# Sink attention and two mixture layers on one core: one float32r product for the sinks, one more Strassen pair, other queues at both ends

## The chip, the core and the metric

The kernel runs on one core of a Trainium2 chip. TensorE (PE) multiplies matrices into PSUM, VectorE (DVE) and ScalarE (ACT) work elementwise on SBUF and PSUM, GpSimd (POOL) elementwise on SBUF alone, and SyncE (SP) issues DMAs; ScalarE and GpSimd can issue DMAs too. The metric is the device time of one execution in microseconds.

## What is computed

Per head of 64 columns, 768 positions attend to the first 4 positions (the sinks) and to a causal window of 128; two layers with different activations follow, each of two products. Everything is float32.

```python
scores = scale * np.matmul(q, k.transpose(0, 1, 3, 2))       # (2, 8, 768, 768)
keep = is_sink | in_window                                    # pos < 4, or 0 <= rel < 128
scores = np.where(keep, scores, -1000000000.0)
a = softmax(scores); attn = np.matmul(a, v)
x = attn.transpose(0, 2, 1, 3).reshape(B * S, H * D)          # 1536 x 512
h = x @ w_in                                                  # 512 -> 2048
g = np.where(h >= 1, h, np.where(h <= -1, 0.0, (h + 1) ** 2 / 4))
x = g @ w_out                                                 # 2048 -> 512
h = x @ w2_in; g = h * np.clip(h + 3.0, 0.0, 6.0) / 6.0
out = g @ w2_out
```

## The kernel before

**Precision.** The large products run in float32r, which streams one column per step but keeps fewer bits than float32. So each operand is split into a high part (rounded to float32r) and a low part (what is left), and three products hi x hi, hi x lo and lo x hi are added in PSUM (`product`, line 678; `y_group`, line 857). `high` (line 134) and `low` (line 142) make the parts; for `high`, and for PSUM copies, a planner of costs (`Balance`) picks VectorE or ScalarE when the program is written.

**Order.** The instructions of PE and SP stand in the order in which the program is written (line 915). VectorE, ScalarE and GpSimd are ordered by a scheduler that simulates the timeline; `keep_in_program_order` pins single instructions, and `tick`/`defer` put pieces of work some steps later.

**Attention** (`build_fast_attention`, line 346). Queries go in blocks of 128. A unit is one block of one pair of heads; 48 units in 16 pieces `j` (4 groups times 4 head pairs). `score` (line 421) multiplies q and k on PE in float32, VectorE adds the mask and takes the maximum (line 444), ScalarE takes the exponential with its sum (line 478). After every second unit `normalise` (line 454) inverts the sums of both units (four columns: two units, two heads) and scales the four probability tiles in place: three on GpSimd (line 469), the fourth on ScalarE or VectorE (lines 471, 473); only in the last four units two or more leave GpSimd. From the third block of a batch on a tile has 260 columns: the block before, 4 sink columns, the block itself. There VectorE first writes the scaled sink columns of the four tiles to `psk` (line 459, 128 x 16). Four units later `turn` (line 500) transposes the probabilities on PE, `sinks` (line 518) transposes `psk` to 8 rows (2 heads times 4 sinks), and `mix` (line 526) multiplies: first the sinks, `vs` against `tsink` in float32 (line 536), then the blocks (line 552). `vs` holds the sinks' rows of v, 8 x 1024, zero where a row belongs to the other head; `load_sinks` (line 400) clears and loads it with four DMAs on SP. Twelve of the 16 `mix` calls have a sink product: eight with 256 columns, four with 512.

**Layers.** 1536 tokens are three chunks of 512 columns (`c`), the 2048 hidden units 16 blocks of 128 (`fc`), two blocks a pair (`p`). `h_group` (line 705) makes one block of one chunk with 12 products, `y_group` one block's share of the output with 12. In plain pairs all three chunks are made so. In the others (`paired`, line 772; from `PLAIN[m]` on, 2 in both layers `m`) chunk 0 is made so, and chunks 1 and 2 with Strassen's seven half products of six instructions each. That needs sums of weight quarters (`combine`, line 286) and of quarters of x (`combine_x`, line 729, tiles `x32`), split into high and low parts in deferred steps on VectorE and ScalarE; in the second layer ScalarE copies the quarters from PSUM (line 882). The weights come as pairs of 32-bit words and are narrowed by VectorE and ScalarE (`narrow`, line 184). Chunks 1 and 2 of all hidden blocks go to HBM and come back (`spill`, `fetch`); their `y_group` calls end each layer.

**Both ends.** `begin` (line 565) issues the loads of q, k and v on SP, in line 394 and 395 for piece 0 in two parts each; GpSimd makes the identity (line 917) and the masks (line 356). In the last `y_group` calls ScalarE and VectorE take turns in copying four output banks (lines 890, 892), and SP stores each (line 894).

## Time and profile before

| | us |
|---|---|
| median of three runs | 610.7 (610.14 to 611.74) |
| the profiled execution | 610.59 |
| its span, first to last instruction | 608.8 |

The page lists how long each engine was busy, divides the span into slices, and follows the chain of work that ended last back from the last instruction. It gives PE 91% of that chain, ScalarE 4% and VectorE 3%. Attention runs to about 106 us, the first layer to about 352, the second to the end. An engine named behind `<-` is what ended an idle time. Durations of matmuls are longer than their distance, since they are pipelined; the chain shows the distance.

### The profile page before, as it was taken

The page shows a single profiled execution, that of the slowest core. Times are in us where ns is not written, and L with a number is a line of the kernel's source. Part 1 is how long each engine was busy: PE and PEld are TensorE (multiplying, and loading weights), DVE is VectorE, ACT ScalarE, POOL GpSimd, SP SyncE. Part 2 cuts the span into 40 slices and gives each one's busy share as a digit, 9 for nine tenths or more (in the row PEclk, how much of TensorE's full clock was granted, in tenths as well). Part 3 has the DMA queues.
Part 4 walks back from the last instruction along what each step waited for, and adds up shares of the span by engine and source line. Part 5 has one row for each costly group of instructions (what it writes and reads, how often), then busy time and mean ns, then how long its engine had stood idle before and what let it go on. Part 6 is the DMA issues. An engine that isn't in the chain of part 4 may idle for free.

```text
span 608.8 us, 8222 instructions
## 1 busy us (share of the span) xinstructions
PE 596.7 (98%) x2880; PEld 478.2 (79%) x2880; DVE 466.4 (77%) x852; ACT 391.3 (64%) x700; POOL 104.8 (17%) x152
## 2 busy tenths in 40 slices
PE   7999899999999999999999999999999999999997
PEld 5666566888888888888888888888888888888885
DVE  5777898899897879477798759787787875666652
ACT  5878888586557576586788666665656554455542
POOL 6666661300111101110000000101011110000000
PEclk9999999999999999999999999999999999999999
DMA  5547501984557586767465204365768554963303
GB/s 180 161 134 237 175 23 70 305 282 155 181 187 229 183 232 180 209 198 252 172 237 212 71 15 159 131 214 153 245 163 242 138 186 129 327 250 138 104 1 139
DMA packets 40571, 106.53 MB, mean 175 GB/s; under 512 B 3409, under 2 KB 13137, under 8 KB 40529
## 3 DMA queue, kind: packets, MB, share of 16 engines
q1 hardware_dynamic: 29776, 72.44, 36.9%
q0 software_dynamic: 10752, 33.56, 17.9%
q8 instruction: 23, 0.38, 0.3%
q14 instruction: 20, 0.16, 0.1%
HBM read 69.29 MB, written 34.60 MB: 171 GB/s over the span
## 4 chain that ended last, share of the span: by engine, by line
PE 91%; ACT 4%; DVE 3%; issue 1%; POOL 0%; DMA 0%; SPq 0%; POOLq 0%; ACTq 0%
PE ps_y L874 43%; PE ps_h L682 40%; ACT p L478 3%; PE ps_s L431 2%; PE ps_v L552 2%; DVE p L444 1%; PE ps_t L515 1%; PE ps_v L536 1%; PE ps_t L514 1%; ACT pt L496 0%; DVE xl L145 0%; POOL p L469 0%; DMA kraw<-k_dram 0%; DVE xh L140 0%; PE ps_k L523 0%
## 5 line engine op out<-in xcount | busy, mean ns | idle before, releaser
L874 PE MATMUL ps_y<-gh,wo 128*128 128x512 f32 x768 | 241.8, 390 | 0.0
L874 PEld LDWEIGHTS ps_y<-gh,wo 128*128 128x128 f32 x768 | 144.2, 188 | 29.8
L682 PE MATMUL ps_h<-xh,wi 128*128 128x512 f32 x480 | 155.1, 391 | 0.0
L874 PE MATMUL ps_y<-gl,wo 128*128 128x512 f32 x384 | 149.7, 390 | 0.0
L682 PEld LDWEIGHTS ps_h<-xh,wi 128*128 128x128 f32 x480 | 90.2, 188 | 19.0 <-issue 0.3
L682 PE MATMUL ps_h<-xl,wi 128*128 128x512 f32 x240 | 93.5, 390 | 0.0
L874 PEld LDWEIGHTS ps_y<-gl,wo 128*128 128x128 f32 x384 | 72.1, 188 | 15.4 <-DVE gl L145 0.4
L469 POOL TENSOR_SCALAR p<-p,sm 128x260 f32<-128x260 f32 (+2 forms) x68 | 58.1, 870 | 33.3 <-DVE psk L459 14.7
L138 ACT ACTIVATE gh<-r 128x512 fp32r<-128x512 f32 x64 | 40.1, 629 | 29.3 <-PE ps_y L874 29.2
L478 ACT ACTIVATE p<-p,nm 128x260 f32<-128x260 f32 (+2 forms) x96 | 46.3, 483 | 17.9 <-DVE nm L444 17.7
L145 DVE TENSOR_TENSOR gl<-r,gh 128x512 fp32r<-128x512 f32 x64 | 43.9, 690 | 17.6 <-ACT gh L138 17.4
L682 PE MATMUL ps_h<-xt,st 128*128 128x512 f32 x216 | 52.9, 389 | 0.0
L682 PEld LDWEIGHTS ps_h<-xl,wi 128*128 128x128 f32 x240 | 45.1, 188 | 9.3
L682 PEld LDWEIGHTS ps_h<-xt,st 128*128 128x128 f32 x216 | 40.6, 188 | 8.4
L697 POOL DMA_DIRECT2D h_d<-hq x32 | 17.8, 556 | 136.4 <-ACT hq L138 88.7
L444 DVE CUSTOM_DVE_ANT_0 p<-ps_s,mask 128x260 f32<-128x260 f32 (+2 forms) x96 | 34.5, 396 | 5.4 <-POOL mask L363 3.8
L662 ACT ACTIVATE r<-hq,half 128x512 f32<-128x512 f32 x32 | 22.8, 723 | 24.4 <-DVE gl L145 18.6
L431 PE MATMUL ps_s<-kraw,qraw 64*128 64x260 f32 (+2 forms) x192 | 31.9, 433 | 4.3 <-DMA kraw<-k_dram 4.0
L663 DVE SCALAR_TENSOR_TENSOR r<-r,hq 128x512 f32<-128x512 f32 x32 | 21.8, 691 | 18.5 <-ACT r L662 18.5
L272 POOL DMA_DIRECT2D wo_d<-w x16 | 8.6, 535 | 155.9 <-DVE w L224 155.8
L797 DVE TENSOR_TENSOR hq<-ps_h,p 128x512 f32<-128x512 f32 x36 | 24.8, 688 | 10.6 <-PE ps_h L682 10.4
L145 DVE TENSOR_TENSOR gl<-ps_h,gh 128x512 fp32r<-128x512 f32 x32 | 22.0, 689 | 13.0 <-ACT gh L138 12.9
(104 smaller groups left out, 927.4 us busy)
## 6 DMA issues: line engine op xcount, KB each, us to landing
h_d<-hq POOLq DMA_DIRECT2D x32, 512.0 KB, 6.0
hq<-h_d SPq DMA_DIRECT2D x32, 512.0 KB, 5.5
wo_d<-w POOLq DMA_DIRECT2D x16, 512.0 KB, 7.2
raw1i<-moe_w_in_dram SPq DMA_DIRECT2D x8, 1024.0 KB, 6.9
wr<-wo_d SPq DMA_DIRECT2D x16, 512.0 KB, 4.9
raw1o<-moe_w_out_dram SPq DMA_DIRECT2D x8, 1024.0 KB, 5.6
raw0i<-moe_w_in_dram SPq DMA_DIRECT2D x7, 1024.0 KB, 6.3
raw0o<-moe_w_out_dram SPq DMA_DIRECT2D x7, 1024.0 KB, 5.8
```

Of the source, the lines that this page charges most:

```text
L138: nc.scalar.activation(out=dst, in_=src, func=AF.Copy)
L145: nc.vector.tensor_tensor(out=dst, in0=src, in1=f32(hi), op=ALU.subtract)
L431: nc.tensor.matmul(banks[e], tq[rows, u * P:(u + 1) * P], tk[rows, c0:c0 + w], start=True, stop=True)
L444: nc.vector.tensor_tensor_reduce(out=p[:, e, :], in0=banks[e], in1=masks[min(i, 2)], scale=-SCALE, scalar=BIG, op0=ALU.add, op1=ALU.min, a ...
L469: nc.gpsimd.tensor_scalar_mul(out=px, in0=px, scalar1=r)
L478: nc.scalar.activation(out=p[:, e, :], in_=p[:, e, :], func=AF.Exp, scale=-1.0, bias=nm[:, v + e:v + e + 1], accum_out=sm[:, v + e:v + e + 1],
L662: nc.scalar.activation(out=r, in_=h, func=AF.Relu, scale=1.0 / 6.0, bias=half)
L663: nc.vector.scalar_tensor_tensor(out=g, in0=r, scalar=1.0, in1=h, op0=ALU.min, op1=ALU.mult)
L682: nc.tensor.matmul(ps, a[:, kc, :], b[kc], start=start and i == 0, stop=i == len(ops) - 1, skip_group_check=not start,)
L697: nc.gpsimd.dma_start(out=h_d[m][fc // 2][:, e:e + 2, :], in_=t)
L797: nc.vector.tensor_tensor(out=dst, in0=src, in1=p1, op=ALU.add)
L874: nc.tensor.matmul(ys[dm], a[:, cs], b, start=fc == 0 and i == 0, stop=last and i == 2)
```

## The change

- **Sinks.** The sink rows of v are loaded in three copies per head (24 rows), split once by VectorE (`split_sinks`, a new step) into rows hi, hi, lo. GpSimd instead of VectorE scales the sink columns to `psk` and then writes `psk3` with hi, lo, hi for each tile. The transposes take 24 columns, and the sink product of `mix`, unchanged in its code, is one float32r product of 24 rows.
- **Strassen.** `PLAIN` of the second layer is 1 instead of 2, so its pair `p=1` is `paired`. Two of the four x32 tiles of that layer take buffers of the tag of the narrowed weights.
- **Start.** The two k transfers of piece 0 are issued by ScalarE. GpSimd's work is put in written order: masks, identity, clearing the sinks.
- **End.** The last output bank is copied in halves by ScalarE and VectorE, and stored in halves by ScalarE's and SP's queues.

```diff
-PLAIN = (2, 2)
+PLAIN = (2, 1)
...
                 nc.sync.dma_start(out=tq[:, part], in_=qs[:, part])
-                nc.sync.dma_start(out=tk[:, part], in_=ks[:, part])
+                (nc.scalar if j == 0 else nc.sync).dma_start(out=tk[:, part], in_=ks[:, part])
...
-        vs = at_p.tile([2 * NS, B, DM], F32, name="vs", bufs=1)
+        R = 6 * NS
+        vs = at_p.tile([R, B, DM], F32R, name="vs", bufs=1)
+        third = at_p.tile([P, 1], F32, name="third", bufs=1)
+        vraw = []
 
         def load_sinks():
-            nc.gpsimd.memset(vs, 0.0)
             for b in range(B):
+                t = g_p.tile([P, N], F32, tag="r", name="vsraw", bufs=3)[:R, :DM]
+                vraw.append(t)
+                nc.gpsimd.memset(t, 0.0)
                 for e in range(2):
                     nc.sync.dma_start(
...
+                        out=t[3 * e * NS:3 * (e + 1) * NS, :].rearrange("r (h e d) -> r h e d", e=2, d=D)[:, :, e, :],
+                        in_=v[b, 0:NS, :].rearrange("s (h e d) -> s h e d", e=2, d=D)[:, :, e, :]
+                        .unsqueeze(0).to_broadcast([3, NS, H // 2, D]),
                     )
+
+        def split_sinks():
+
+            nc.vector.tensor_reduce(
+                out=third, in_=ident[:, :R].rearrange("p (e x s) -> p e x s", e=2, x=3)[:, :, 2, :], axis=AX.XY, op=ALU.add
+            )
+            nc.vector.tensor_scalar_mul(out=third, in0=third, scalar1=-1.0)
+            for b in range(B):
+                hi = g_p.tile([P, N], F32R, tag="gh", name="vshi", bufs=3)[:R, :DM]
+                tc.keep_in_program_order(nc.vector.tensor_copy(out=hi, in_=vraw[b]))
+                tc.keep_in_program_order(
+                    nc.vector.scalar_tensor_tensor(
+                        out=vs[:, b, :], in0=f32(hi), scalar=third[:R], in1=vraw[b], op0=ALU.mult, op1=ALU.add
+                    )
+                )
...
-                    nc.vector.tensor_tensor(
+                    ps3 = at_p.tile([P, 4, 3, NS], F32R, tag="psk3", name="psk3", bufs=DIST // 2 + 2)
+                    nc.gpsimd.tensor_tensor(
                         out=ps, in0=p4[:, :, P:KB], in1=sm.unsqueeze(2).to_broadcast([P, 4, NS]), op=ALU.mult
                     )
...
+                if w > 2 * P:
+                    nc.gpsimd.tensor_copy(
+                        out=ps3[:, :, 0:3:2, :], in_=ps.unsqueeze(2).to_broadcast([P, 4, 2, NS])
+                    )
+                    nc.gpsimd.tensor_tensor(out=ps3[:, :, 1, :], in0=ps, in1=f32(ps3[:, :, 0, :]), op=ALU.subtract)
...
-                nc.tensor.transpose(ps[0:2 * NS, n, :], both[:, 2 * NS * n:2 * NS * (n + 1)], ident)
+                nc.tensor.transpose(ps[0:R, n, :], both[:, R * n:R * (n + 1)], ident)
...
             load(0)
-            prepare()
             load_v(0)
             load(1)
             load_v(1)
             load(2)
+            with tc.manual_schedule(engines={mybir.EngineType.Pool}):
+                prepare()
+                make_identity(nc, ident)
             load_sinks()
...
+            if g == 4:
+                steps.append(split_sinks)
...
+        if m and i < 2:
+            if ("a", i) not in x32s:
+                x32s["a", i] = raw_p.tile([P, HK, N], F32, tag="wi32", name=f"x32_{i}", bufs=2)
+            return x32s["a", i]
...
+                        final = c == NCH - 1 and dm == KC - 1
+                        if final:
+                            nc.scalar.activation(out=od[:, :N // 2], in_=ys[dm][:, :N // 2], func=AF.Copy)
+                            nc.vector.tensor_copy(out=od[:, N // 2:], in_=ys[dm][:, N // 2:])
...
+                if m and final:
+                    nc.scalar.dma_start(out=out[cs, c * N:c * N + N // 2], in_=od[:, :N // 2])
+                    nc.sync.dma_start(out=out[cs, c * N + N // 2:(c + 1) * N], in_=od[:, N // 2:])
```

## Rows read from the trace of the kernel before

**Rows 1.** The page's busy line: each engine's busy us, share of span, instructions
```profile
PE 596.7 (98%) x2880; PEld 478.2 (79%) x2880; DVE 466.4 (77%) x852; ACT 391.3 (64%) x700; POOL 104.8 (17%) x152
```

**Rows 2.** Stages: stretch, length, busy us (instructions) per engine, PE clock, DMA, GB/s
```profile
10.00:20.00 10.00, 10.00 (x59) 6.84 (x60) 8.07 (x38) 7.56 (x30) 7.95 (x11) 1.00 0.48 161
...
70.00:80.00 10.00, 10.00 (x80) 6.63 (x78) 8.55 (x33) 7.60 (x26) 8.54 (x10) 1.00 0.15 45
...
90.00:100.00 10.00, 10.00 (x61) 7.20 (x60) 9.54 (x26) 8.29 (x22) 1.77 (x2) 1.00 0.26 105
...
362.00:373.00 11.00, 11.00 (x51) 9.09 (x50) 10.76 (x11) 7.55 (x10) 1.48 (x3) 1.00 0.13 50
```

**Rows 3.** Chain that ended last, whole span: start us, length us, what
```profile
17.58 0.62 PE ps_v L536 x2
...
66.98 2.76 POOL p L469 x3
...
103.48 1.05 PE ps_v L536 x2
...
365.43 2.72 PE ps_y L874 x12
...
604.83 0.69 DVE o L892
```

**Rows 4.** Groups, 5 to 106.4 us, by form: busy us, mean ns | idle before
```profile
L469 POOL TENSOR_SCALAR p<-p,sm 128x260 f32<-128x260 f32 x44 | 41.2, 952 | 26.3 <-DVE psk L459 14.7 <-ACT p L478 7.4 <-ACT pts L496 2.3
...
L469 POOL TENSOR_SCALAR p<-p,sm 128x128 f32<-128x128 f32 x16 | 9.8, 619 | 7.0 <-ACT p L478 3.4 <-PE ps_s L431 2.5 <-ACT pt L496 0.8
...
L536 PE MATMUL ps_v<-pts,vs 8*128 8x256 f32 x16 | 5.4, 419 | 1.4 <-DVE pts L498 0.6 <-ACT pts L496 0.3 <-DVE xl L145 0.3
...
L536 PE MATMUL ps_v<-pts,vs 8*128 8x512 f32 x8 | 4.5, 640 | 0.0
...
L459 DVE TENSOR_TENSOR psk<-p,sm 128x16 f32<-128x16 f32 x16 | 3.2, 202 | 0.4
...
L138 ACT ACTIVATE xh<-ps_v 128x256 fp32r<-128x256 f32 x5 | 1.9, 371 | 0.0
...
L140 DVE CAST wi<-w 128x512 fp32r<-128x512 f32 x2 | 1.1, 557 | 0.1
```

**Rows 5.** Groups, whole span: one scalar-tensor-tensor of VectorE
```profile
L663 DVE SCALAR_TENSOR_TENSOR r<-r,hq 128x512 f32<-128x512 f32 x32 | 21.8, 691 | 18.5 <-ACT r L662 18.5
```

**Rows 6.** Timeline of the start: start us, us, engine, line, op [idle <-releaser]
```profile
0.73 1.28 ACT L478 ACT_TABLE_LOAD   x1 [0.73 <-PEq L1041]
...
2.11 0.43 SPq L395 DMA_DIRECT2D kraw<-k_dram  x1
...
4.50 0.09 POOL L363 MEMSET mask<- 128x4 f32 x1
...
4.79 1.39 PEld L431 LDWEIGHTS ps_s<-kraw,qraw 64*128 64x128 f32 x8 [1.09 <-DMA qraw<-q_dram]
4.83 5.50 PE L431 MATMUL ps_s<-kraw,qraw 64*128 64x256 f32 x20 [0.83 <-DMA kraw<-k_dram]
```

**Rows 7.** Timeline of GpSimd, 60 to 100 us: its longest run
```profile
66.98 8.24 POOL L469 TENSOR_SCALAR p<-p,sm 128x260 f32<-128x260 f32 x9 [3.01 <-ACT p L478]
```

**Rows 8.** Waits, 5 to 106.4 us: total us, times, longest us
```profile
PEld ps_t L514 <- POOL p L469: 4.8, 10, 0.7
```

**Rows 9.** Timeline of VectorE, 352 to 405 us: last two low parts xt
```profile
372.20 1.22 DVE L145 TENSOR_TENSOR xt<-x,xt 128x1024 fp32r<-128x1024 f32 x1
...
383.37 1.23 DVE L145 TENSOR_TENSOR xt<-x,xt 128x1024 fp32r<-128x1024 f32 x1 [0.81 <-ACT xt L138]
```

**Rows 10.** Timelines of ScalarE, then VectorE, 345 to 358 us
```profile
347.11 1.96 ACT L138 ACTIVATE xh<-ps_y 128x512 fp32r<-128x512 f32 x3 [2.77 <-PE ps_y L874]
348.96 0.59 ACT L882 ACTIVATE x<-ps_y 128x512 f32<-128x512 f32 x1
...
347.74 2.06 DVE L145 TENSOR_TENSOR xl<-ps_y,xh 128x512 fp32r<-128x512 f32 x3 [2.67 <-ACT xh L138]
```

More of the change, by code (lines that the diff above doesn't have):

```diff
@@ L522, in sinks @@
             for n, u in enumerate(us):
[L523 to L524 removed]
+                nc.tensor.transpose(ps[0:R, n, :], both[:, R * n:R * (n + 1)], ident)
+            copy(pt[j][1][:, us[0]:us[-1] + 1, :], ps[0:R, :len(us), :], len(us) * P)
         def mix(j):
@@ L916, in sink_attention_moe_moe_kernel @@
         nc.vector.memset(half, 0.5)
-        make_identity(nc, ident)
+        if not fast:
+            make_identity(nc, ident)
         if fast:
```

26 lines of the change are left out of this document (12 added, 14 removed).

## The prediction

> **What bounds the kernel now.** I read the page's busy line first, then the stages, then the chain of work that ended last, and only then the groups and single stretches of the timeline. The busy line puts TensorE at 98% of a span of 608.8 us [rows 1], but a busy PE means two different things here. From the end of the attention, near 106 us, to 604.8 the chain is PE alone, twelve 512-column products per 2.72 us, that is 0.2267 us each, without a hole [rows 3]; what counts there is the number of products. In the attention before it PE is marked busy at 10.00 of 10 us (its ends are modelled), while VectorE and ScalarE stand at 75 to 95% and GpSimd between 18 and 85% [rows 2]. There the chain changes hands between PE, VectorE, ScalarE and once GpSimd (2.76 us at 66.98) [rows 3], so four engines pass one piece of work around, and a saving on one counts only until the next is late. The granted clock is 1.00 in every stage, the 2.4 GHz level [rows 2]; no part of the sum rests on it. The profiled execution took 610.59 us for its span of 608.8; the median of the three timed runs is 610.7. I sum against 610.59 and add 0.1 at the end.
>
> **Strassen pair.** In the second layer the pair p=1 goes from plain to paired. Plain it costs six groups of 12 products, 72; paired it is 24 for chunk 0 and 7 x 6 = 42 for the other two, 66. Six products less at 0.2267 us [rows 3] give -1.36 us on an engine that is the chain. What covers it: the operands xt come from VectorE, and before, their last but one low part ends at 373.4 and the last at 384.6 [rows 9]. Counting products from the y group at 365.43 [rows 3] (then h of chunk 2, then the pair), the paired p=1 wants the first of these at 379 and the last at 390. Cover of 5 us each, on a VectorE that is 98% busy from 362 to 373 but has nothing due earlier [rows 2]. The pair adds three additions of 0.69 us in place of copies, and its weight combination moves into the end of layer one. Two x32 tiles move to the buffers of the narrowed weights, which are idle then. If the cover failed, at most the 1.36 us would be lost. I take -1.36.
>
> **Start.** Two k transfers move from SP's queue to ScalarE's. Unit 1 begins at 4.83: its k was issued at 2.11 as fourth of four and is last, but q, issued one slot before, is waited for to 4.79 as well [rows 6]. So not both slots come back: q moves up by one issue of 0.43 us [rows 6] and k by two. GpSimd now finishes the three masks before the identity and the memsets; VectorE's first pass waited for the mask write at 4.50 [rows 6], and that moves ahead of the scores. SP's later loads of v, q, k also move up by two slots. I take -0.45. Bounds: -0.9, two slots, and +0.3, if ScalarE loads its table first (1.28 us from 0.73 [rows 6]) so that k is issued at 2.0 and 2.45 instead of 1.18 and 2.11.
>
> **The product of the sinks on PE.** Twelve products of 8 rows in float32 take two passes each: on the chain 0.62 us for a pair of 256 columns and 1.05 for one of 512 [rows 3]; there are 16 and 8 instructions [rows 4]. In float32r one pass is left: 512 columns for 0.2267 us, and 256 for 0.12 to 0.23 (no row shows them; I take 0.12, half of 512). In all 8 x (0.65 - 0.12) + 4 x (1.05 - 0.23) = 7.5 us less PE work. The transposes grow from 8 to 24 columns of weights; they move the same 128 columns, so I cost them at nothing (the weight loads lie beside matmuls). But only seven of the twelve lie on the chain, from 17.58 to 103.48 [rows 3], four of 256 columns and three of 512: 4 x 0.52 + 3 x 0.82 = 4.5 us. The last three stand after 84 us, where PE is dense to the end of attention and the next deadline of VectorE has slack; of their 2.46 I count 2.0. In the middle, with ScalarE and VectorE at 75 to 90%, I count half of 2.1. Sum -3.0, bounds -4.6 and -1.0.
>
> **VectorE.** The scaling of sink probabilities leaves it: 16 x 0.202 = 3.2 us [rows 4]. It is worth something only where VectorE is nearly full, in the eight pairs after 60 us; half of their 1.6: -0.8 (bounds -3.2 and 0). The split of v's sinks comes on, in program order behind the scores of step 4, near 11 us: a reduction and a scaling on tiny shapes (0.2 each, after psk), two casts at 0.557 [rows 4] and two scalar-tensor-tensor at 0.691 [rows 5], 2.9 us. Queued behind it are masks and PSUM copies that PE's transposes wait for. VectorE has 1.9 us free between 10 and 20 us [rows 2], so +1.0; bounds 0 and +2.9. Its four loads write three copies of each row and wait for two memsets of GpSimd; behind them on SP stand only the loads of q and k three pairs ahead, so I cost these at nothing.
>
> **GpSimd.** Per sink pair three new instructions (product, copy of 32, difference of 16) stand ahead of the three scalings, 48 in all. No row shows them. From above: the scalings cost 952 ns for 260 columns and 619 for 128 [rows 4], a line that meets 16 columns at 0.34 us; three make 1.05. From below: the shortest GpSimd row, a memset of 4 columns at 0.09 [rows 6], three make 0.27. I take 0.8, nearer the line, since these too read operands; 16 pairs make 13 us. It does not all count: GpSimd is idle between pairs, and it no longer waits for VectorE's psk. But at 66.98 it runs nine scalings end to end, 8.24 us [rows 7], and PE's transposes wait for it ten times [rows 8]; three sink pairs stand in that run, and two in the next, so 5 x 0.8 = 4 us can show, against PE and VectorE work that got shorter there. I take +1.5, bounds 0 and +5; no gain, since the three stand ahead of the scalings and are longer than the 0.2 us of psk that these waited for.
> The fourth scaling (VectorE or ScalarE) now must wait for GpSimd's product, as it overwrites what that reads. This is an added wait; masks and PSUM copies queue behind it. It costs nothing where GpSimd is free when the sums are ready.
> The Trainium skill, GPSIMD Engine Reference, section Engine selection, advises against this move: elementwise two-input work is about twice as slow there as on VectorE. By twice psk's 0.202 us an instruction would be 0.4 us and the three 1.2, an estimate from that page, above my upper bound; no run here shows it yet.
>
> **The end.** The last bank is copied by VectorE in 0.69 us [rows 3] and stored. Halved, ScalarE takes 0.37 for 256 columns [rows 4] and VectorE about as much. Side by side this gives -0.3. But in layer one, where both engines read the same bank, ScalarE's plain copy starts at 348.96 although the first of its three evictions from 347.11 on was over by 347.8; VectorE reads that bank from 347.74 to about 348.4 [rows 10]. One after the other the halves take 0.37 + 0.4, +0.1, with the first half's store ahead and the second one half as long. I take 0.0, bounds -0.35 and +0.1.
> The Trainium skill, PSUM — Partial Sum Buffer, section on PSUM bank collisions, says that ScalarE and VectorE must not read one bank at a time, so that software has to order them. By that rule the halves run one after the other; the trace agrees in the order at 348.96, and the sum is the same to 0.1 us.
>
> **Sum.** -1.36 - 0.45 - 3.0 - 0.8 + 1.0 + 1.5 + 0.0 = -3.1 us; 610.59 - 3.1 = 607.5, and 607.6 against the median.
>
> **Rivals.** (A) The forecast, 607.6, own range 604.8 to 608.8.
> (B) GpSimd takes PE's place: PE's transposes wait for it in the five crowded pairs for the whole 4 us, and the split costs its 2.9. Then 610.6 - 3.1 + 2.5 + 1.9 = 611.9, or with half of that 609.7: no change to be measured. For it: the nine scalings in a row. Against it: GpSimd stood 3.0 us ahead of that run [rows 7], and it is on the chain only once.
> (C) Slower: the fourth scaling behind GpSimd's queue. Place: VectorE's and ScalarE's in-order queues between 40 and 88 us. A pair's three scalings take 2.75 us; whenever the next pair's sums are ready while they run, the engine stands for what is left. Five pairs run into each other like this (two in the run of nine [rows 7], three in shorter runs of six), so up to 13.8 us, half of it 6.9: 610.6 - 3.1 + 6.9 = 614.4. It outweighs the rest from 3.1 us of such standing on, and shows from 5.0. For it: the runs without pause. Against it: the order of VectorE and ScalarE is planned with this dependency known, and other work can be put ahead.
> (D) PE is the bound throughout: the whole chain share passes, 4.6 instead of 3.0, the split hides, GpSimd costs nothing: 610.6 - 1.36 - 0.45 - 4.6 - 0.8 = 603.4. For it: PE busy 10 of 10. Against it: what ScalarE and VectorE hold in the same chain.
> (E) The Strassen pair doesn't do what it says: VectorE, full at 362 to 373, is late with the operands and PE stands for the 1.36 us: 609.0.
>
> **How the numbers follow.** A 0.48, D 0.12, B 0.22, E 0.05, C 0.13. A difference of 0.3%, 1.8 us, is about what a measurement of this kernel can tell from no change: faster is below 608.9, slower above 612.5. A and D are faster, 0.60; B and E the same, 0.27; C slower, 0.13. The range runs from 603.0 (all of D) to 612.5, over B whole and the cheap end of C's mechanism, and leaves out most of C and what might lie below D.
>
> **What would show it.** Right, if L874's first block starts about 2 us earlier, and from there to the end the distance shrinks by 1.4 us; if the sink products show 12 instructions; if unit 1's scores start near 4.4; if the transposes' wait for GpSimd grows by no more than some 2 us. Wrong, if VectorE or ScalarE stand before their scaling with GpSimd as releaser (C), if attention is no shorter (B), if holes appear in PE between 365 and 395 us (E), or if the attention is shorter by 5 us or more (D).

## The result and the profile after

The changed kernel is slower: 615.67 us median (612.59 to 618.27) against 610.79 us of the kernel before (610.14 to 611.85), a ratio of 1.0071 with a 95% interval of 1.0054 to 1.0087. The forecast was 607.6 us in a range of 603.0 to 612.5, so it had the wrong sign and the range missed. The times also lie further apart than before, 5.7 us against 1.7, and the mean granted clock of each execution goes with them: 612.59 and 613.76 us at 1.000, 615.19 at 0.997, 616.15 and 616.76 at 0.994, 618.23 and 618.27 at 0.992, and one against the order, 614.74 at 0.991. So some 2.5 us of the 4.9 go with the clock and 2.4 us are there without it, an estimate from the two at 1.000 (mean 613.2). The profiled run took 616.15 us with a span of 614.0, that is 5.2 us more span than before.

The busy line of the page of the changed kernel (each engine's busy us, share of the span, instructions), which answers to [rows 1]:

```profile
PE 596.0 (97%) x2862; PEld 477.3 (78%) x2862; DVE 468.7 (76%) x850; ACT 392.1 (64%) x702; POOL 119.6 (19%) x202
```

PE was busy 596.7 us in the shorter run, so the 5.2 us are not work. The stages, as in [rows 2] (stretch, length, busy us and instructions of PE, PEld, VectorE, ScalarE and GpSimd, PE clock, DMA share, GB/s), show a granted clock below 1.00, which before has in no stage, and a PE that is idle in stages through which it was busy before (10.00 of 10 us, 13.00 of 13):

```profile
10.00:20.00 10.00, 8.93 (x42) 5.45 (x42) 9.42 (x43) 5.87 (x22) 6.35 (x13) 1.00 0.34 111
60.00:70.00 10.00, 8.08 (x53) 5.36 (x54) 7.16 (x33) 7.00 (x24) 4.99 (x9) 0.83 0.57 188
70.00:80.00 10.00, 8.85 (x67) 5.64 (x69) 8.09 (x38) 9.16 (x32) 9.71 (x18) 1.00 0.36 101
130.00:143.00 13.00, 10.52 (x40) 8.23 (x39) 13.00 (x17) 11.63 (x14) 2.12 (x2) 0.87 0.54 182
```

Between 60 and 70 us PE was idle before too. The same view of before has a stage that [rows 2] left out:

```profile
60.00:70.00 10.00, 8.16 (x66) 5.27 (x63) 8.71 (x44) 8.94 (x32) 5.84 (x8) 1.00 0.79 255
```

PE's timeline has the places (start us, us, engine, line, operation, idle before and who ended it): the first transposes, the first hole, the first y block of layer one, and the second hole.

```profile
13.16 0.69 PE L542 MATMUL ps_t<-ident,p 128*128 128x128 f32 x2
...
63.76 1.16 PE L579 MATMUL ps_v<-pt,vraw 128*64 128x256 f32 x8 [1.92 <-DMA vraw<-v_dram]
...
114.51 0.39 PE L909 MATMUL ps_y<-gh,wo 128*128 128x512 f32 x1
...
139.14 0.68 PE L909 MATMUL ps_y<-gl,wo 128*128 128x512 f32 x1 [2.48 <-DVE gl L145]
```

Behind both holes the products take about twice their time (0.68 against 0.39 for one of 512 columns) until 67.5 and 142.7 us: the 1.2 GHz level. By the stages it cost 10 x (1 - 0.83) = 1.7 and 13 x (1 - 0.87) = 1.7 us. The second hole opens where the chain of before ran without one. There VectorE had made gl, the low part that the second product of the block reads, just in time; its and then PE's timeline of before at this place:

```profile
132.82 0.69 DVE L145 TENSOR_TENSOR gl<-ps_h,gh 128x512 fp32r<-128x512 f32 x1
```
```profile
133.75 0.39 PE L874 MATMUL ps_y<-gh,wo 128*128 128x512 f32 x1
133.98 0.39 PE L874 MATMUL ps_y<-gl,wo 128*128 128x512 f32 x1
```

gl was ready at 133.51 and wanted at 133.98: half a microsecond. In the changed kernel VectorE's planned order has three more operations ahead of it:

```profile
136.06 0.69 DVE L203 TENSOR_SCALAR w<-w 128x1024 f32<-128x1024 f32 x1
136.66 0.69 DVE L210 TENSOR_SCALAR raw0i<-raw0i 128x1024 int32<-128x1024 int32 x1
137.26 1.22 DVE L783 TENSOR_TENSOR x<-x,x 128x1024 f32<-128x1024 f32 x1
138.40 0.69 DVE L145 TENSOR_TENSOR gl<-ps_h,gh 128x512 fp32r<-128x512 f32 x1
```

The chain that ended last, which in before is PE alone from 106 us on, now has no PE between 102.26 and 139.14 us. It goes back from gl over VectorE, ScalarE and once GpSimd (1.29 us), which are preparing weights, and over one transfer of weights:

```profile
110.41 8.45 DMA wo_d<-w
...
138.40 0.70 DVE gl L145
```

At the start VectorE stands for the loads of the sinks, and the masks of unit 3 come behind the split (its timeline):

```profile
9.56 0.71 DVE L423 CAST vshi<-vsraw 24x512 fp32r<-24x512 f32 x1 [1.08 <-DMA vsraw<-v_dram]
10.20 0.41 DVE L465 CUSTOM_DVE_ANT_0 p<-ps_s,mask 128x260 f32<-128x260 f32 x1
10.54 0.07 DVE L465 DVE_READ_ACCUMULATOR2_ANT nm<- 128x1 f32 x1
10.54 0.73 DVE L425 SCALAR_TENSOR_TENSOR vs<-vshi,third,vsraw 24x512 fp32r<-24x512 f32 x1
```

The first transposes were at 10.25 before and are at 13.16. The profiled runs by stage, read from PE's timelines ("eighth" is the eighth sink product of twelve; "layer one" is what a kernel loses against before between its first y block and the y block at 163.99 of before):

| kernel | first sink product at | to the eighth | to the ninth | to the twelfth | first y at | lost in layer one |
|---|---|---|---|---|---|---|
| before | 17.51 | 38.87 | 19.87 | 27.16 | 111.99 | 0 |
| changed | 20.19 | 35.90 | 22.52 | 27.41 | 114.51 | 4.08 |
| e1 (sinks undone) | 17.15 | 38.72 | 19.85 | 27.18 | 111.46 | 0.11 |
| e17 (one pass alone) | 18.54 | 35.10 | 20.37 | 26.41 | 108.95 | 1.98 |
| e18 (split alone) | 20.66 | 38.74 | 21.21 | 27.10 | 116.26 | 0.15 |
| e3 (sink work on VectorE) | 19.82 | 36.80 | 19.65 | 26.67 | 111.45 | 1.46 |
| e2 (weights later) | 19.83 | 35.89 | 20.89 | 27.40 | 112.54 | 4.03 |

The changed kernel's sum against before: +2.68 at the start, -2.97 from the first to the eighth sink product, +2.65 to the ninth (the first hole and its slow clock), +0.25 and -0.09 to the first y, +4.08 in layer one (the second hole, its slow clock), -1.36 for the Strassen pair; 5.2 us.

### The profile page after: what moved, and what is told of

Same layout as the page of the kernel before. It is cut to its first block, busy times and chain, and to the rows that moved or that the text cites. A ratio compares the mean times of both kernels' runs of the same rounds, so it can differ in the third digit from the quotient of the medians.

```text
span 614.0 us, 8246 instructions
## 1 busy us (share of the span) xinstructions
PE 596.0 (97%) x2862; PEld 477.3 (78%) x2862; DVE 468.7 (76%) x850; ACT 392.1 (64%) x702; POOL 119.6 (19%) x202
## 4 chain that ended last, share of the span: by engine, by line
PE 83%; DVE 6%; POOL 4%; DMA 3%; issue 2%; ACT 2%; SPq 0%; POOLq 0%; DVEq 0%; ACTq 0%
PE ps_y L909 42%; PE ps_h L713 36%; POOL p L496 3%; PE ps_v L579 2%; DVE p L465 1%; DMA wo_d<-w 1%; PE ps_s L452 1%; DMA vraw<-v_dram 1%; PE ps_t L541 1%; PE ps_t L542 1%; DMA vsraw<-v_dram 1%; DVE w L224 1%; ACT p L505 1%; ACT w L198 0%; DVE x L783 0%
## 5 line engine op out<-in xcount | busy, mean ns | idle before, releaser
L713 PE MATMUL ps_h<-xh,wi 128*128 128x512 f32 x456 | 147.8, 391 | 0.0
L713 PEld LDWEIGHTS ps_h<-xh,wi 128*128 128x128 f32 x456 | 85.6, 188 | 18.0 <-issue 0.3
L713 PE MATMUL ps_h<-xl,wi 128*128 128x512 f32 x228 | 88.9, 390 | 0.3 <-DVE xl L145 0.3
L496 POOL TENSOR_SCALAR p<-p,sm 128x260 f32<-128x260 f32 (+2 forms) x68 | 59.9, 893 | 5.6 <-ACT p L505 2.7
L505 ACT ACTIVATE p<-p,nm 128x260 f32<-128x260 f32 (+2 forms) x96 | 46.3, 483 | 18.6 <-DVE nm L465 17.4
L713 PE MATMUL ps_h<-xt,st 128*128 128x512 f32 x234 | 57.3, 389 | 0.0
L713 PEld LDWEIGHTS ps_h<-xt,st 128*128 128x128 f32 x234 | 43.9, 188 | 9.1
L713 PEld LDWEIGHTS ps_h<-xl,wi 128*128 128x128 f32 x228 | 42.8, 188 | 9.5 <-DVE xl L145 0.7
L452 PE MATMUL ps_s<-kraw,qraw 64*128 64x260 f32 (+2 forms) x192 | 34.3, 443 | 5.5 <-DMA kraw<-k_dram 3.9
L832 DVE TENSOR_TENSOR hq<-ps_h,p 128x512 f32<-128x512 f32 x39 | 26.8, 688 | 13.1 <-PE ps_h L713 13.0
L694 DVE SCALAR_TENSOR_TENSOR r<-r,hq 128x512 f32<-128x512 f32 x32 | 21.8, 691 | 18.6 <-ACT r L693 18.5
L452 PEld LDWEIGHTS ps_s<-kraw,qraw 64*128 64x128 f32 x192 | 20.1, 213 | 14.1 <-DVE nm L465 5.4
```

The costliest lines, as they stand in the source:

```text
L452: nc.tensor.matmul(banks[e], tq[rows, u * P:(u + 1) * P], tk[rows, c0:c0 + w], start=True, stop=True)
L496: nc.gpsimd.tensor_scalar_mul(out=px, in0=px, scalar1=r)
L505: nc.scalar.activation(out=p[:, e, :], in_=p[:, e, :], func=AF.Exp, scale=-1.0, bias=nm[:, v + e:v + e + 1], accum_out=sm[:, v + e:v + e + 1],
L694: nc.vector.scalar_tensor_tensor(out=g, in0=r, scalar=1.0, in1=h, op0=ALU.min, op1=ALU.mult)
L713: nc.tensor.matmul(ps, a[:, kc, :], b[kc], start=start and i == 0, stop=i == len(ops) - 1, skip_group_check=not start,)
L832: nc.vector.tensor_tensor(out=dst, in0=src, in1=p1, op=ALU.add)
```

## The experiments

Fifteen kernels ran. They are given in the order of the argument: which part costs, then the two holes, the clock, and where the saving goes. Ratios are to the kernel before, run on the same chip, and differences "by the ratios" are differences of two such ratios times 610.8 us.

**Undo the sinks.** The 8-row product, VectorE's scaling and the plain loads are put back; the pair, the first k by ScalarE and the halved last bank stay.

```diff
-                nc.tensor.transpose(ps[0:R, n, :], both[:, R * n:R * (n + 1)], ident)
+                nc.tensor.transpose(ps[0:2 * NS, n, :], both[:, 2 * NS * n:2 * NS * (n + 1)], ident)
...
-                steps.append(split_sinks)
```

> The changed kernel with the whole part of the sinks put back (8-row float32 products, VectorE scales the sink columns, no split, no extra GpSimd work); the Strassen pair, the first k by ScalarE, the order of GpSimd at the start and the halved last bank stay. All theories that blame the sinks (two holes in PE with a slow clock behind each; GpSimd; the split on VectorE at the start) expect before minus 1.36 us of the pair and 0 to 0.3 of the start: 609.2 to 609.5. If one of the other parts caused the loss, it stays: 612 or more. The y group of layer one starts near 112 and 133.9 us as in before, and no stretch shows a clock below 1.00.

Measured: 608.96 us (608.80 to 609.52), ratio 0.997 (0.9957 to 0.9983). The loss is in the sinks' part, and this kernel beats both others. The granted clock is 1.00 in every stage.

**The split alone.** The same kernel, with the 24-row loads, the memsets and the split put in as work that nothing reads; the sinks' own loads come after the scores of step 2.

```diff
...
+            if g == 2:
+                steps.append(load_sinks)
+            if g == 4:
+                steps.append(split_sinks)
```

> The cost of the split by itself: the kernel with the sinks undone, with the 24-row loads, the two memsets and the split of v's sinks (2.6 us of VectorE in all) added at the places that they have in the changed kernel; nothing reads what they make, and the sinks' own four loads come behind the scores of pair 0. Theory: VectorE stands for the loads near 8.5 us and then holds the masks of unit 3 back, so the first transposes start near 13 instead of 10.06, the first sink product near 19.9 instead of 17.15, and all of it reaches the first y of layer one, since nothing behind it has slack: 113.9 to 114.3, time 611 to 612. Rival (VectorE's idle time of the next 30 us takes it back): first y at 111.5 to 112.5, 609 to 610.

Measured: 612.88 us (611.81 to 613.87), ratio 1.0024 (1.0006 to 1.0041), 3.3 us above e1 by the ratios. VectorE's cast and PE's scores behind it, from their two timelines, and a stage:

```profile
10.18 0.53 DVE L434 CAST vshi<-vsraw 24x512 fp32r<-24x512 f32 x1 [1.71 <-DMA vsraw<-v_dram]
```
```profile
11.10 0.71 PE L463 MATMUL ps_s<-kraw,qraw 64*128 64x256 f32 x2 [2.10 <-DVE nm L476]
```
```profile
10.00:20.00 10.00, 8.26 (x37) 5.33 (x38) 9.08 (x38) 5.75 (x21) 5.36 (x7) 0.66 0.30 90
```

VectorE stood 1.71 us for the load, PE 2.10 us for VectorE, and the clock fell behind that. The first y came 4.8 us later than in e1 in this run, the longest of the ten. So 2.6 us of VectorE work cost more than themselves; the rival (idle time takes it back) falls. In the changed kernel VectorE stands 1.08 us for the load, so 3.3 us may be more than the split costs there.

**The one-pass product alone.** e1 with float32r operands of 8 rows, rounded by two ScalarE copies.

```diff
-        vs = at_p.tile([2 * NS, B, DM], F32, name="vs", bufs=1)
+        vs = at_p.tile([2 * NS, B, DM], F32R, name="vs", bufs=1)
+        vf = at_p.tile([2 * NS, B, DM], F32, name="vf", bufs=1)
...
+        def round_sinks(b):
+            nc.scalar.activation(out=vs[:, b, :], in_=vf[:, b, :], func=AF.Copy)
```

> The disputed saving by itself: the kernel with the sinks undone (608.96 us), but the product of 8 rows takes float32r operands and so one pass of PE instead of two (16 of 24 instructions become 12 in one pass); two ScalarE copies of 8x512 round v's sinks, the copies from PSUM round the probabilities. No split into three parts, nothing more on VectorE or GpSimd: the sinks' product is computed with rounded operands, less exactly than the reference asks for in principle. If PE's saving is worth what the stretch from 17 to 56 us showed, the first y of layer one comes 2.5 to 3.5 us earlier than with the sinks undone (111.46): 108 to 109, and the time is 605.5 to 606.5. Rival (the saving is mostly hidden behind VectorE and ScalarE, and the 3 us of that stretch were VectorE's and ScalarE's own order): first y at 110.5 or later, 608 to 609.

Measured: 610.84 us (607.64 to 612.86), ratio 0.9982 (0.996 to 1.0005), no gain over e1 that the intervals show. The profiled run (608.38) shows a part of why: the attention is shorter by the 2.5 us, first y at 108.95, but layer one takes 1.98 us back. PE, then VectorE, at the second hole's place:

```profile
132.20 0.50 PE L886 MATMUL ps_y<-gl,wo 128*128 128x512 f32 x1 [1.11 <-DVE gl L145]
```
```profile
130.33 1.22 DVE L145 TENSOR_TENSOR xt<-x,xt 128x1024 fp32r<-128x1024 f32 x1
131.47 0.68 DVE L145 TENSOR_TENSOR gl<-ps_h,gh 128x512 fp32r<-128x512 f32 x1
```

gl stands right behind xt here, as in before; VectorE is without a pause from 130 us on and PE comes 2.5 us earlier than in e1, so PE waits. This run had the clock at 1.00 and is 2.5 us below the median, so it can't explain the whole. The three executions with a mean granted clock of 0.998 or more took 608.27 to 609.71 us; of the seven below, five took more than 611. The slow clock has a share in the lost saving too; where it falls in those seven no profile here shows.

**The sink operations on VectorE.** The changed kernel with its three GpSimd operations of a pair moved.

```diff
-                    nc.gpsimd.tensor_tensor(
+                    nc.vector.tensor_tensor(
                         out=ps, in0=p4[:, :, P:KB], in1=sm.unsqueeze(2).to_broadcast([P, 4, NS]), op=ALU.mult
...
-                    nc.gpsimd.tensor_copy(
+                    nc.vector.tensor_copy(
...
-                    nc.gpsimd.tensor_tensor(out=ps3[:, :, 1, :], in0=ps, in1=f32(ps3[:, :, 0, :]), op=ALU.subtract)
+                    nc.vector.tensor_tensor(out=ps3[:, :, 1, :], in0=ps, in1=f32(ps3[:, :, 0, :]), op=ALU.subtract)
```

> The changed kernel with the three sink operations of a pair (scaling, copy of 32 columns, difference) on VectorE instead of GpSimd. GpSimd theory: PE's waits for GpSimd's probabilities in 64 to 106 us (12.0 us in sum against 6.0 before) shrink to 6 and the stretch from the PE hole to the first y of layer one, 45.7 us in both kernels, gets shorter by 2 us or more: below 613 with the hole still there. Theory of the two holes: that stretch keeps its 45.7 within 0.7 us; the order of VectorE behind it is another (gl stands ahead of the narrowing again), so the second hole is small and the time is 610.5 to 612.5 with the first hole in, 609 if that goes too.

Measured: 610.80 us (610.12 to 612.21), ratio 1.0000 (0.9991 to 1.001): 4.3 us less than the changed kernel by the ratios, and the times lie within 2.1 us. Neither theory had it whole. GpSimd's price is there, but small where it works: from the eighth to the twelfth sink product 46.3 us against 48.3 in e2, which has no hole at 62 us either. The rest goes with VectorE's order, which has gl ahead of the three operations again (the wait for it is 0.58 us), and with the hole at 62 us, which is 0.71 us.

**The weights later.** The 1 MB load between q, k and v at 53 us is moved to a quiet time.

```diff
-                    if left == 60:
+                    if left == 44:
                         load_w(0, "i", 1)
```

> The changed kernel with one edit: the 1 MB load of the first layer's second weights, issued at 53.3 us between loads of q, k and v, is issued 8 pairs of units later (near 67 us), where the DMA queues are idle. Theory of the two holes: PE's hole at 61.8 to 63.7 us was v behind these weights, and with it go 1.9 us of waiting, less the 0.6 that before waits there too, and 1.7 us lost at the 1.2 GHz level behind it: about 2.9 us, so 612.8; attention ends near 111.6 instead of 114.5, and the second hole (136.6 to 139.1) stays. GpSimd theory and theory of the split at the start: 615.7 as it was, since neither is touched; the PE hole would then move or the time be lost again before 100 us.

Measured: 615.07 us (614.02 to 617.68), ratio 1.0071 (1.0047 to 1.0096). In the profiled run the hole at 62 us is gone and the first y comes 2.0 us earlier, so v was late behind the weights; but the median does not move (five executions). The two stages (same columns as above):

```profile
60.00:70.00 10.00, 8.53 (x63) 5.57 (x62) 8.11 (x41) 9.02 (x33) 6.54 (x13) 1.00 0.72 234
...
130.00:143.00 13.00, 10.49 (x40) 8.08 (x39) 13.00 (x17) 11.07 (x14) 0.63 (x1) 0.87 0.44 163
```

The second hole (2.51 us) and its clock stay.

**gl first.** The narrowing of the fourth pair's first weights keeps its place in program order, and VectorE makes gl right behind xt.

```diff
-            keep = spread or (m, which, p) not in ((0, "i", 2), (0, "o", 2), (0, "i", 3), (0, "o", 3))
+            keep = spread or (m, which, p) not in ((0, "i", 2), (0, "o", 2), (0, "o", 3))
```

> The changed kernel with one edit: the narrowing of the fourth pair's first weights keeps its place in program order, so that VectorE makes gl of layer one's third block right after xt, and not behind three operations of 0.60, 0.60 and 1.13 us. Theory of the two holes: the second hole (PE 136.6 to 139.1, 2.5 us, then 3.4 us at the 1.2 GHz level) goes, about 4.2 us: 611.5. Rival, that the hole comes from the DMA transfers that made VectorE late (0.75 us more behind than the attention): the order alone gives back at most the 2.3 us of the three operations, and the clock still falls: 613.4. GpSimd or start theory: nothing here, 615.7.

Measured: 615.40 us (611.34 to 619.85), ratio 1.0066 (1.0032 to 1.0101). In the profiled run (612.62) the hole is 0.46 us with the clock at 1.00 behind it, but a hole of 1.26 us comes up at 149 us behind ScalarE, and the clock falls in another place, behind a hole of 1.65 us at the start:

```profile
10.00:20.00 10.00, 8.96 (x42) 6.09 (x42) 9.59 (x42) 6.27 (x23) 6.35 (x13) 0.66 0.32 111
```

That fall cost nothing against the changed kernel, whose PE is not at full pace before 16.5 us either (last section): the first sink product is at 20.15 here and at 20.19 there. The profiled run is 2.8 us below the median; the two executions with a mean granted clock of 1.000 took 611.62 and 612.47 us, the one at 0.991 took 619.85. The theory that the two holes of one profiled run are the loss is too narrow.

**One hole filled, then three.** Work that nothing reads is put into PE's queue where it waits: first at the second hole alone, then at the start and at 62 us too.

```diff
+                if (m, fc, c, dm, i) == (0, 2, 0, 0, 1):
+                    dead = bank_h()
+                    for x in range(10):
+                        nc.tensor.matmul(dead, hi[:, cs], gh, start=True, stop=True)
...
+            if j == 9:
+                fill(14)
...
+                steps.insert(len(steps) - 2, lambda: fill(8))
```

> The changed kernel with ten products of 512 columns added that nothing reads, put in PE's queue between the first and the second product of layer one's third y block, that is into the hole in which PE waits 2.48 us for gl. Theory that the clock falls because PE stood still: the hole is filled (10 x 0.227 = 2.3 us), gl comes as late as before, but the stretch behind it stays at 1.00 instead of 3.4 us at the 1.2 GHz level: 1.7 us shorter in this place, though 2.3 us of work are added; the time is 614 where the other places behave as they did. Rival, that the clock falls for another reason (the DMA load, the power of the other engines): the granted clock of 130 to 143 us stays at 0.87 and the time is 615.7 to 616.

> The changed kernel with work that nothing reads in PE's queue at three of its holes: 8 transposes of the identity ahead of the scores that wait for VectorE near 10.7 us, 14 ahead of the product that waits for v near 61.8, and the ten products of 512 columns behind gh at 136. About 1.7, 1.5 and 2.3 us of PE work more. Theory that the holes matter mostly through the 1.2 GHz stretches behind them, which come in some runs and not in others: the granted clock stays at 1.00 in 10 to 20, 60 to 70 and 130 to 143 us, the times lie within 3 us of each other and the median is 612.5 to 614, in spite of the added work. Rival (the spread comes from GpSimd or the DMA queues): spread of 5 us and more as before, median 615.5 or more.

Measured with one: 614.73 us (612.98 to 616.99), ratio 1.0057 (1.0041 to 1.0073); the clock behind the filled hole is 1.00, where the changed kernel had 0.87. With three: 612.94 us (612.10 to 614.53), ratio 1.0034 (1.002 to 1.0048). The three stages of the latter:

```profile
10.00:20.00 10.00, 10.00 (x49) 6.87 (x49) 8.77 (x40) 5.83 (x22) 6.56 (x11) 1.00 0.32 99
60.00:70.00 10.00, 9.98 (x82) 7.36 (x80) 7.86 (x39) 7.64 (x26) 6.40 (x11) 1.00 0.73 243
...
130.00:143.00 13.00, 13.00 (x60) 10.74 (x59) 13.00 (x16) 10.18 (x13) 0.53 (x1) 1.00 0.39 145
```

About 5 us of PE work more, 2.3 us less time by the ratios, and a spread of 2.4 us (seven executions) in place of 5.7 (eight). At 62 and 136 us the 1.2 GHz stretches behind the waits are gone. At the start the filling brought nothing: whatever the clock column reads there, the transposes come every 0.21 us up to 17.4 us, and the first sink product is at 20.23 against 20.19. With the times by clock in the section on the result this says that the slow stretches make most of the spread, and the rival (GpSimd or DMA queues) falls as far as the spread goes.

**The split apart.** The second batch's split comes behind the scores of step 12. The text on record describes a larger edit than the kernel that ran: there the loads and the first batch's split kept their places.

```diff
-                steps.append(split_sinks)
+                steps.append(lambda: (split_third(), split_sinks(0)))
+            if g == 12:
+                steps.append(lambda: split_sinks(1))
```

> The changed kernel with the split of v's sinks taken apart: the two loads of the first batch behind the scores of pair 0, its cast and difference (1.4 us) behind the first transposes' copies near 13 us instead of at 9.6, where VectorE stood 1.08 us for the load; the second batch's near 45 us. The rest is as it was, GpSimd and both later holes too. Theory: the split held the masks of unit 3 back, so the first transposes start at 10.5 instead of 13.16 and the first sink product at 18 instead of 20.19; attention keeps 2 us of it unless the hole at 62 us (v behind the weights) takes it, because PE gets there earlier than the data: then the hole grows from 1.9 to 3 to 4 us. Time 613.5 to 615. Rival (the 2.7 us at the start are the loads' and the masks' order, not the split): first sink product stays near 20, 615.7.

Measured: 612.90 us (611.01 to 615.23), ratio 1.0023 (1.0007 to 1.004), 2.9 us less than the changed kernel by the ratios. The first transposes come at 12.12, the first y at 111.08, and the second hole takes 2.88 us with the clock at 0.87 behind it.

**Combinations.** With the split apart: gl first as well (e13), and then the sink operations on VectorE too (e15). With the first batch's loads behind the scores of step 2 and its split behind step 6, the second batch's behind steps 16 and 24, and with the later weights: sink operations on VectorE (e9), on GpSimd with gl first (e10). Their diffs are those above.

> The changed kernel with the second batch's split behind the scores of step 12 (first y of layer one at 111.08 instead of 114.51 in the run that did this alone) and with gl of layer one's third block ahead of the narrowing (the hole there 0.5 us instead of 2.9, with no slow clock behind it). Theory that the changed kernel loses its time in these two places and not by its GpSimd work: first y near 111.1, the hole small: 607.5 to 609.5, faster than before. If GpSimd's work or the DMA hole is what makes its times spread from 611 to 619, the median stays at 611 or more.

> As the run before, but with the three sink operations of a pair on VectorE instead of GpSimd. GpSimd theory: about 1 us better than the run before (608 against 609), and its times lie as close together as those of the run that moved only these operations (610.1 to 612.2); theory of the two places alone: equal to the run before within 0.5 us and the same spread.

> Three repairs in one: split taken apart as in the run before, the three sink operations of a pair on VectorE instead of GpSimd, and the 1 MB of weights loaded near 67 us instead of 53. Sum theory: the sink product alone is worth 3 us of PE time between 17 and 56 us (first to ninth sink product 38.9 us before, 35.9 after), and only what stood against it took that back; the first y block of layer one starts at 109.2 to 110 (111.99 before, 111.45 with the operations on VectorE alone), the hole behind it is below 0.6 us: 606.5 to 607.5, faster than the kernel with the sinks undone (608.96). Rival (VectorE is the next bound, the saving of PE is lost to it in 56 to 106 us): first y at 111 to 111.5, 608.5 to 609.5, no better than undoing the sinks.

> As the run before, but the sink operations stay on GpSimd, and the narrowing of the fourth pair's first weights keeps its place in program order (so that gl is not behind it). GpSimd theory: from 67 to 85 us GpSimd runs without a gap, 3.4 us for a sink pair instead of 2.75, so PE's transposes wait for it and 1.2 to 2 us are lost against the run before, whatever comes ahead of it; what PE gained up to 60 us is lost there too: first y at 111.5 to 112.5, time 609.5 to 611. Theory of the two holes alone (GpSimd costs nothing by itself): first y near 109.5 to 110, time 607 to 608.

(The "ninth" in the third text is the eighth.) Measured: e13 613.60 us (609.32 to 617.28), ratio 1.0036 (1.0004 to 1.0069); e15 613.30 (612.24 to 615.69), 1.0030 (1.0012 to 1.0048); e9 612.35 (611.21 to 614.05), 1.0023 (1.0009 to 1.0037); e10 612.98 (611.89 to 620.01), 1.0053 (1.0019 to 1.0087). None came down to the time that was expected. e15 lies 0.3 us from e13, as the theory of the two places had it, but its times lie closer together (3.5 us against 8.0), as the GpSimd theory had it. In e13, profiled in its longest run, the second hole is 0.28 us, and one of 3.26 us opens 17 us further on, where PE waits for ScalarE:

```profile
152.09 0.50 PE L715 MATMUL ps_h<-xh,wi 128*128 128x512 f32 x1 [3.26 <-ACT p L829]
```

In e9 the second sink product comes at 27.84, 1.3 us later than the changed kernel's. Repairs do not add up here. The likely reason is that each one makes the planner order VectorE and ScalarE anew, and both are nearly full; no run isolates this.

**Where the saving goes.** The one-pass kernel with the weights later, and as control e1 with the same edit.

> The kernel with the one-pass product alone (median 610.84, 607.6 to 612.9), with the 1 MB of weights loaded near 67 us instead of 53. The sinks' product is computed with rounded operands, as there. Theory that PE, being earlier by 2.5 us, runs into transfers that did not come earlier: the hole of 1.76 us at 61 us goes, the times close up, and what is left of the saving behind layer one's first blocks (1.1 us in the profiled run of 608.38) shows in the median: 606.5 to 608. Rival (the saving is lost in layer one's first blocks whatever happens ahead of them): 608.5 to 609.5, equal to the kernel with the sinks undone.

> Control: the kernel with the sinks undone (608.96), with the same load moved to 67 us. There PE waits for v only 0.6 us or less, so little is to be had: 608.3 to 609.1, the times as close together as they were (608.8 to 609.5). If it gets as much faster as the kernel with the one-pass product does, the load is a matter of its own and has nothing to do with the saving.

Measured: e20 610.72 us (608.38 to 613.04), ratio 0.9994 (0.9976 to 1.0012); its profiled run showed a granted clock of 0.95 from 30 us to the end, so only its times are used. e21 610.80 (609.38 to 612.61), ratio 1.0003 (0.9992 to 1.0015). The saving does not show, and the control got 2.0 us slower by the ratios. The load's old place was the better one. In the control's profiled run (610.43) the first y is 0.65 us later than in e1, and layer one loses 1.0 us more; why the move does that is open. The clock has a part here too: five executions at 0.998 or more took 609.38 to 610.43 us, the five below 611.16 to 612.61.

## Why the prediction was wrong

**The bound of layer one.** The step that failed first is in the opening part: from 106 us on "the chain is PE alone, [...] without a hole [rows 3]; what counts there is the number of products". The chain told who was last, not by how much. At 133.98 gl had been ready for half a microsecond, on a VectorE that is busy 13.00 of 13 us there. In the changed kernel VectorE's order differs by three operations, and 4.08 us were lost where the sum had nothing: 2.48 us of waiting and 1.7 us of slow clock behind it make nearly all of it. With the order of before the wait can open too. In e17, whose attention is 3.04 us shorter, PE waits 1.11 us for gl and layer one loses 1.98; in e3, 0.54 us shorter, it waits 0.58 and loses 1.46; in e21, whose first y is 0.12 us late, it waits 0.42 and loses 1.10; in e18, 4.27 us late, it does not wait and loses 0.15. So an early PE opens it, and a late VectorE does as well. VectorE as the bound there fits these waits and the chain; it was not tried by making VectorE lighter.

**The clock.** That "no part of the sum rests on it" was the second slip. All stages of before stood at 1.00, with no hole above 0.83 us behind the first scores. In the changed kernel two stretches at 1.2 GHz cost 1.7 us each, and e19 took them away by filling holes. The sum and the range had no term for this, nor for a spread of 5.7 us.

**Split on VectorE, +1.0 (0 to +2.9).** Mis-sized: up to 3.3 us by itself (e18 against e1). That its four loads were costed at nothing was the slip: their issues alone took 3.29 us of SP's queue from 4.75 us on, VectorE stood 1.08 us for them, and the masks of unit 3 behind it are what PE waited for. The 1.9 us of VectorE's idle time were no cover, because the work stands in order ahead of masks that were due.

**Product on PE, -3.0 (-4.6 to -1.0).** The attention gave about that: -2.97 us between the first and the eighth product, -2.5 at the first y in e17. The parts were off. The groups of PE (as in [rows 4]) have twelve instructions, as foreseen:

```profile
L563 PE MATMUL ps_v<-pts,vs 24*128 24x256 f32 x8 | 3.0, 380 | 0.0
...
L563 PE MATMUL ps_v<-pts,vs 24*128 24x512 f32 x4 | 2.0, 497 | 0.0
```

On the path 256 columns took 0.31 us (20.19 to 20.50) and 512 took 0.43 (106.02 to 106.45), not 0.12 and 0.23: 8 x 0.31 + 4 x 0.62 = 5.0 us of work saved instead of 7.5. More of it passed in the early products and less in the last ones than assumed. What failed is the step from attention to total: nothing of it is in the median (e17), where layer one and the clock took it. And PE was less dense in the attention than the prediction read it: the 10.00 of 10 us hold for the three attention stages that it shows, from 60 to 70 us it was 8.16.

**GpSimd, +1.5 (0 to +5).** The three operations, by form in the attention (busy us, mean ns):

```profile
L489 POOL TENSOR_TENSOR psk<-psk,psk 128x16 fp32r<-128x16 f32 x16 | 4.2, 262 | 0.0
L486 POOL CAST psk<-psk 128x32 fp32r<-128x32 f32 x16 | 4.1, 255 | 1.0
L481 POOL TENSOR_TENSOR psk<-p,sm 128x16 f32<-128x16 f32 x16 | 3.5, 216 | 15.8 <-DVE sm L477 10.7 <-ACT p L505 4.4 <-ACT pts L523 0.7
```

0.73 us for the three, estimate 0.8. The run of nine scalings [rows 7] became five sink pairs end to end, 3.4 us each where before took 2.75; the first of them and the start of the second on GpSimd's timeline:

```profile
67.66 0.22 POOL L481 TENSOR_TENSOR psk<-p,sm 128x16 f32<-128x16 f32 x1 [3.82 <-DVE sm L477]
67.94 0.21 POOL L486 CAST psk<-psk 128x32 fp32r<-128x32 f32 x1
68.13 2.75 POOL L496 TENSOR_SCALAR p<-p,sm 128x260 f32<-128x260 f32 x3
70.85 0.22 POOL L489 TENSOR_TENSOR psk<-psk,psk 128x16 fp32r<-128x16 f32 x1
71.17 0.21 POOL L481 TENSOR_TENSOR psk<-p,sm 128x16 f32<-128x16 f32 x1
```

In the attention it cost 1.1 us (first y of e2 against e3), near the sum's 1.5; in the median 4.3 us (changed kernel against e3), as the order of VectorE and the holes came with it. How much of the 4.3 is order and how much GpSimd's own is open. The stated sign, that the transposes' wait for GpSimd grows by no more than some 2 us, failed; the waits (total us, times, longest) answer to [rows 8], where the first was 4.8:

```profile
PEld ps_t L541 <- POOL p L496: 8.6, 17, 1.1
PE ps_t L541 <- POOL p L496: 3.4, 8, 0.8
PE ps_v L579 <- DMA vraw<-v_dram: 1.9, 1, 1.9
...
DVE p L500 <- POOL psk L481: 0.8, 2, 0.4
ACT p L498 <- POOL psk L481: 0.7, 1, 0.7
```

Most of this growth is not the three operations' doing: with them on VectorE (e3) the first two rows are 7.0 and 3.2 us. The last two rows are rival C's added wait: 1.5 us in all, far from its 6.9. So C had the sign but not the mechanism, and that its 614.4 is the number nearest to the measured one is luck. In mechanism rival B (609.7 to 611.9) was nearest, with the split at its full 2.9 and GpSimd on PE's path; its price stopped at the attention. The page's rule weighed in the prediction (the Trainium skill, GPSIMD Engine Reference, Engine selection: two-input work about twice as slow there) is not what this size shows: the product and the difference took 216 and 262 ns on GpSimd, 174 and 184 on VectorE in e3. What the three add to the queue of scalings, 0.65 us a pair, is more than that difference.

**VectorE's scaling off, -0.8.** Not to be told apart from the rest: with it back and two operations more (e3) the stretch to the eighth product is 0.9 us longer than in the changed kernel, the later ones shorter.

**Start, -0.45.** In e1 the first y is 0.53 us earlier, which fits. But unit 1's scores began at 4.72 in the changed kernel instead of the 4.4 of the stated sign, and anywhere from 4.35 to 5.51 in the sixteen profiled runs with this start, since they wait for the second part of k. That k moves up by two slots holds for the issue (0.72 us), not for the landing. And PE came to full pace at 13.4 us in e1 and at 15.5 in before (last section), so a part of the 0.53 can be the clock's.

**Strassen pair, -1.36.** Right. Distance to before: 6.60 us at the start of layer two (h at 351.83 before, 358.43 after), 5.24 at the last y run (515.03 and 520.27). The chain has no hole there, and the last low parts of xt (VectorE's timeline, as in [rows 9]) keep their cover in a kernel that is 6.6 us late:

```profile
378.80 1.22 DVE L145 TENSOR_TENSOR xt<-x,xt 128x1024 fp32r<-128x1024 f32 x1
389.68 1.22 DVE L145 TENSOR_TENSOR xt<-x,xt 128x1024 fp32r<-128x1024 f32 x1
```

**The end, 0.0.** Right: 4.0 us from PE's end to the span's end, before and after. The halves run one after the other, as the rule on PSUM bank collisions has it (the Trainium skill, PSUM — Partial Sum Buffer); the trace agrees, from the chain:

```profile
520.27 89.79 PE ps_y L909 x396
610.09 0.39 ACT o L927
610.50 0.42 DVE o L928
```

## What to carry to other kernels

Where the chain shows one engine alone, look at how long its operands have been ready at each of its groups; a place with half a microsecond of slack can be a second bound, and a saving ahead of it, or a new order of the engine that makes them, can be lost there. A part that goes in front of due work on an in-order engine costs its wait and everything queued behind it, so time its load first. When PE is fed by a nearly full engine, a hole can cost more than its length, since a slow clock may follow. Judge a change by several runs and their clocks, because one profile shows only where that run's holes fell.

## What the runs showed of the hardware

PE's granted clock fell to the 1.2 GHz level behind holes of 1.92 and 2.48 us in the changed kernel, 1.65 in e7, 2.10 in e18 and 2.51 in e2, and the products behind the holes ran at half pace for a while (0.68 us for 512 columns against 0.39 in the changed kernel). The length of one hole does not decide it. No fall followed the holes of 2.41 us in e15 and 1.76 us in e17 (rows of their PE timelines); the eight products behind them take the 0.87 us that such eight take elsewhere at full pace:

```profile
64.48 0.87 PE L579 MATMUL ps_v<-pt,vraw 128*64 128x256 f32 x8 [2.41 <-DMA vraw<-v_dram]
```
```profile
61.15 0.87 PE L556 MATMUL ps_v<-pt,vraw 128*64 128x256 f32 x8 [1.76 <-ACT p L482]
```

And in e18 the clock fell at 73 us (0.51 from 73.0 to 76.5) behind three holes of 0.47 to 0.68 us. What decides is not shown here. With the holes at 62 and 136 us filled by work that nothing reads the clock stayed at 1.00 there (e19), and the kernel became faster with about 5 us more work.

At the start PE's transposes come every 0.21 us and later every 0.11. The change comes at about 13.4 us in e1, 15.5 in before, 16.5 in the changed kernel and 17.4 in e19, while the granted clock reads 1.00 on both sides of it; there the durations tell more than the clock column. In e7 and e18, where the column reads 0.66 for 10 to 20 us, it comes at about 18.2 and 18.5.

The load of v (128 KB) that PE waited for at 62 us took 6.7 us to land in the changed kernel (issued at 56.89) and 6.3 in before (issued at 56.63), both with q, k and 1 MB of weights under way; in e2, where the weights go later, it took 2.9. The issue of k just ahead of it took 1.04 us in the changed kernel and 0.48 in before.
